# Scatter indices converted one column at a time on ScalarE, and a different pacing of the side work, in an FNet + mixture-of-experts kernel

## The chip, the cores and the metric

The kernel runs on one core of one Trainium2 chip. The metric is the device time in microseconds (us) of that core, the median of three executions without the profiler. A further execution was recorded by the hardware profiler; everything called "the profile" or "the trace" here is that one execution. Its engines are named PE (TensorE, matrix multiplication), PEld (its weight loads), DVE (VectorE), ACT (ScalarE), POOL (GpSimd) and SP (the queue that issues plain DMAs).

## The reference

Two blocks follow each other. The first takes the real part of a two-dimensional Fourier transform of each of eight sequences. The second is a dropless mixture of experts: every row goes to the expert with the largest gate logit, through that expert's two layers, and the result is scaled by the gate's probability.

```
x: (8, 2496, 256)              w_gate: (256, 8)   w1: (8, 256, 1024)   w2: (8, 1024, 256)
X = real(fft(fft(x, axis=1), axis=2)).reshape(19968, 256)
logits = X @ w_gate
e = argmax(logits, 1);  gate = softmax(logits)[row, e]
out[row] = gate * (relu(X[row] @ w1[e]) @ w2[e])
```

All arithmetic is float32.

## The kernel before

**The transform** works batch by batch (b = 0 to 7). `first(b)` folds the input, multiplies it on PE (tile `s`), copies it with ACT (L316) and writes it to a DRAM buffer `Td`. `second(b)` reads it back, makes twice ten tiles of 128 rows in two halves (h = 0, 1), and computes the gate logits beside them; its DVE and ACT steps are L374 to L405.

**Routing.** After each half, `route(b, h)` (L411) finds each row's expert and its place in a DRAM buffer `Xs`, where each expert has a region of its own. The place is made on DVE: `pf` is the float result (L447), and L448 adds a constant that pushes unwanted rows out of bounds and converts to integers, in the tile `pi` (128 x 10, one column for each tile of 128 rows). The ten (index column, row tile) pairs of a half are put in the list `waiting`.

**Scatters.** `send()` takes one pair from that list and issues one indirect DMA on POOL's queue (L230), which writes 128 rows of 1032 bytes to `Xs`. There are 20 for each batch, 160 in all. Results go out through the same queue, and the same line: one indirect DMA `out_dram<-y,ro` for each 128 finished rows.

**The experts.** `experts` takes blocks of rows of one expert from `Xs`: 256 or 128 rows for batches 0 and 1, 512 rows later, at the end 256 and 128 again. `plan(b, ...)` computes on DVE which rows and which expert each block has (tile `p_tab`, L479 to L512); it runs after a batch's last scatter was issued in program order. `fetch` (L517) reads that table into SP's registers and issues three loads: the rows `xb` (L522), which also need the scatters of the batch to have landed, and the expert's two weight matrices. The second layer of a block is eight matmuls for each 128 rows into `py`, evicted by ACT to `y` (L702), then the outgoing DMA. The first layer is a matmul into `ph` with ACT and DVE taking turns to evict it (L684, L682). For 512-row blocks of batches 3 and later (`halved`, L190) the first layer is instead `seven` (L577), which forms a product of 2 x 2 blocks from seven products in place of eight. It has two groups of seven steps, about 0.86 us of PE each; its PSUM tiles `a` and `c` are written twice in a group, so that the second product into `a` waits for ACT's copy L597, and the second into `c` for DVE's L606.

**Order of the work.** All queues are in the order in which the Python code emits instructions; no scheduler changes it. The loop at L804 weaves two generators. `work` (the experts, on the blocks of batch b-1) reports after each piece how much PE work it was (`w`, in units of four 256-wide float32 matmuls, about 1.73 us) and whether it was a piece of `seven` (`full`). `side` is the transform of batches b and b+1, routing and `plan`. Pieces that are not `full` add `TICKS * w / (SHARE * open_)` to `due`, and for each whole unit of `due` the side work moves one step; `SHARE` is thus the part of the round's pieces over which 32 side steps are spread. In rounds b < 4 (`LATE`) each side step is followed by a `send()`. In rounds b >= 4 `send()` is called from L823: `room` grows by `w` with every piece, `full` or not, and each scatter takes `ROOM` = 1.2 from it. A side step that finds `waiting` not yet empty does nothing more than let the next batch's `first` run; `plan` begins once it is empty.

Of the kernel before, what the change touches and what calls it, by code (L numbers as in the profile page):

```python
# [15 lines left out]
ALU = mybir.AluOpType  # L16
# [34 lines left out]
def bc(ap, axis, n):  # L51
    shape = list(ap.shape)
    shape.insert(axis, n)
    return ap[tuple([slice(None)] * axis + [None])].to_broadcast(shape)
# [77 lines left out]
def rounds():  # L132

    want = [((256, 2), (128, 4)), ((256, 4),)] + [((512, B),)] * (B - 2)
    plan, used = [], 0

    def full(done, size):
        return max(0, -(-(done - used - E * (size - 1)) // size))  # L140

    for b in range(B):
        done = (b + 1) * S
        now = []
        for size, most in want[b]:
            k = min(full(done, size), most)
            if k:
                now.append((size, k, False))
            used += size * k
        if b == B - 1:  # L150
            k = full(done, BLK)
            used += BLK * k
            now.append((BLK, k, False))
            now.append((REST, (NT - used + E * (REST - 1)) // REST, True))
        plan.append(now)
    return plan
# [25 lines left out]

TICKS = 32
LATE = 4
SHARE, ROOM = 0.65, 1.2
WARM = 16
MOST = max(k for now in rounds() for _, k, _ in now)

# [1 line left out]
def halved(b, size):  # L190

    return size == 512 and b > 2
# [17 lines left out]
def kernel(ctx: ExitStack, tc, x, w_gate, w1, w2, out):  # L210
    nc = tc.nc
    vec, act, pool = nc.vector, nc.scalar, nc.gpsimd

    def mm(o, lhsT, rhs, start=True, stop=True, **kw):
        nc.tensor.matmul(o, lhsT=lhsT, rhs=rhs, start=start, stop=stop, **kw)  # L215
# [13 lines left out]
    def put_row(dst, idx, rows, last, group):  # L229
        return unordered(pool.indirect_dma_start(  # L230
            out=dst, out_offset=bass.IndirectOffsetOnAxis(ap=idx, axis=0),
            in_=rows, in_offset=None, bounds_check=last, oob_is_err=False), group)


    def sent(ins, b):
        tc.declare_no_dep(ins, group="taken", reason="no block before this batch's round has these rows")
        tc.add_to_no_dep_group(f"xs{b}", ins)
# [25 lines left out]
    con, k = {}, 0  # L263
# [92 lines left out]
    def second(b):  # L356
# [31 lines left out]
        for h in range(2):  # L388
            rows = sp.tile([128, NSL, W], F32, tag="rows", name="rows")
            lg = sp.tile([128, NSL, E], F32, tag="lg", name="lg")  # L390
            for i in range(HW):
                w, k = HW * h + i, 2 * i
                if w + 2 < NG:
                    group(w + 2)
                p3 = pm_.tile([128, 2 * NY + 2 * E + 1], F32, tag="m", name="p3")
                z = zz[:, :, 128 * w:128 * (w + 1)]
                mm(p3[:, 0:NY + 2 * E], z[:, 0], con["rd"][:, 0, 0:NY + 2 * E], True, False, skip_group_check=True)
                mm(p3[:, NY:], z[:, 1], con["rd"][:, 1], False, True, skip_group_check=True)
                zs = sp.tile([128, NY + 1], F32, tag="zs", name="zs")
                act.copy(zs[:], p3[:, NY + 2 * E:])  # L400
                if i:
                    mirror(rows, k - 2)
                vec.tensor_copy(lg[:, k:k + 2], p3[:, NY:NY + 2 * E].rearrange("p (m e) -> p m e", m=2))  # L403
                for m, op in enumerate((ALU.add, ALU.subtract)):
                    vec.scalar_tensor_tensor(rows[:, k + m, 0:NY], p3[:, 0:NY], zs[:, 0:1], zs[:, 1:],  # L405
                                             op0=ALU.add, op1=op)
                yield
            mirror(rows, k)
            yield from route(b, h, rows, lg)

    def route(b, h, rows, lg):  # L411

        nonlocal base

        def small(name, *dims, dt=F32):
            return sp.tile([128, *dims], dt, tag=name, name=name)

        mx, eq, v = small("mx", NSL), small("eq", NSL, E), small("v", NSL)
        vec.reduce_max(mx[:], lg[:], axis=AX_X)
        vec.tensor_tensor(eq[:], lg[:], bc(mx[:], 2, E), op=ALU.is_equal)  # L420
        vec.tensor_tensor(eq[:], eq[:], bc(con["rev"][:], 1, NSL), op=ALU.mult)
        vec.reduce_max(v[:], eq[:], axis=AX_X)
        vec.tensor_tensor(v[:], v[:], con["good"][:, h], op=ALU.mult)
        oh = small("oh", NSL + 1, E, dt=BF16)
        vec.memset(oh[:, NSL], 0.0)
        vec.tensor_tensor(oh[:, 0:NSL], bc(con["rev"][:], 1, NSL), bc(v[:], 2, E), op=ALU.is_equal)
        yield

        su = small("su", NSL)
        vec.tensor_tensor(lg[:], lg[:], bc(mx[:], 2, E), op=ALU.subtract)  # L430
        act.activation(lg[:], lg[:], ACTF.Exp)
        vec.tensor_scalar(rows[:, :, D], con["row"][:, h], float(b * S), None, op0=ALU.add)
        yield

        rk = pm_.tile([128, NSL + 1, E], F32, tag="m", name="rk")
        mm(rk[:], tri[:], oh[:], True, False)
        for s in range(NSL):
            mm(rk[:, s + 1:], ones[:], bc(oh[:, s], 1, NSL - s), False, s == NSL - 1)
        vec.reduce_sum(su[:], lg[:], axis=AX_X)
        vec.tensor_scalar(su[:], su[:], 1e-9, None, op0=ALU.add)  # L440
        vec.reciprocal(rows[:, :, D + 1], su[:])
        yield

        pos, pf, pi = small("pos", NSL, E), small("pf", NSL), small("pi", NSL, dt=I32)
        vec.tensor_tensor(pos[:], rk[:, 0:NSL], bc(base[:], 1, NSL), op=ALU.add)
        vec.tensor_tensor(pos[:], pos[:], oh[:, 0:NSL], op=ALU.mult)
        vec.reduce_sum(pf[:], pos[:], axis=AX_X)  # L447
        vec.tensor_tensor(pi[:], pf[:], con["far"][:, h], op=ALU.add)  # L448
        nxt = cp.tile([128, E], F32, tag="base", name="base", bufs=2)
        vec.tensor_tensor(nxt[:], rk[:, NSL], base[:], op=ALU.add)  # L450
        base = nxt
        for s in range(NSL):
            waiting.append((b, pi[:, s:s + 1], rows[:, s]))

    waiting = deque()

    def send():

        if waiting:
            b, idx, rows = waiting.popleft()  # L460
            sent(put_row(Xs, idx, rows, E * CAP - 1, "xs"), b)


# [255 lines left out]
    def woven(*parts):  # L719
        parts = list(parts)  # L720
        while parts:
            for p in list(parts):
                if next(p, p) is p:
                    parts.remove(p)
                else:
                    yield

    def close(b):

        for size, k, last in rounds()[b]:  # L730
            yield from plan(b, size, k, last)
# [7 lines left out]
    def mixed(b):  # L739

        one, two = (ahead_of(b + 1) if b + 1 < B else iter(())), second(b)
        for _ in range(3):
            next(one, None)
            yield
        for k, _ in enumerate(two):
            if k % 2:
                next(one, None)
            yield
        while waiting:
            next(one, None)  # L750
            yield
        yield from woven(close(b), one)
# [43 lines left out]
    for k, _ in enumerate(second(0)):  # L796
        if k % 2 == 0:
            next(early, None)
        send()
    while waiting:  # L800
        next(early, None)
        send()
    work = experts(todo)
    for b in range(1, B):  # L804

        side, done, due, room = mixed(b), 0, 0.0, 0.0
        if b == 1:
            side = woven(close(0), chain(early, side))
        blocks = [(size, k * size / BIG, halved(b - 1, size)) for size, k, _ in rounds()[b - 1]]
        total = sum(k * (15 if seven_ else 16) for _, k, seven_ in blocks)  # L810
        open_ = sum(k * (8 if seven_ else 16) for _, k, seven_ in blocks)
        while done < total:
            w, full = next(work)
            done += w
            if not full:
                due += TICKS * w / (SHARE * open_) if w else 1
            while due >= 1:
                next(side, None)
                due -= 1
                if b < LATE or not w:  # L820
                    send()
            room = min(room + w, 2)
            if b >= LATE and room >= ROOM:  # L823
                send()
                room -= ROOM
        for _ in side:
            send()
# [52 lines left out]
```

## Time and profile before

| what | value |
|---|---|
| time, three executions | 1330.49, 1332.57, 1944.71 us |
| median | 1332.57 us |
| span of the profiled execution | 1362.3 us |
| mean granted TensorE clock in it | 0.984 |
| rows of PE / DVE / ACT / POOL | 6655 / 1533 / 806 / 335 |
| DMA volume | 249.62 MB, 183 GB/s over the span |

The third execution stands far outside and is used nowhere. In the profiled execution the clock row shows full speed except in a few slices before 380 us, the lowest 0.70 between 68 and 102 us. Each row of the trace gives start and duration of one instruction or of several equal ones (x8), what it writes and reads, and in brackets how long its engine had been idle and what ended the idle time. [...] Matmul ends are modelled, and overlap the next matmul's start.

### The profile page before, as it was taken

The numbers are of one execution on the slowest core, as the hardware profiler recorded it, in microseconds if no ns is written. First come the engines' busy times: TensorE is split into PE (matmuls) and PEld (weight loads), VectorE is DVE, ScalarE is ACT, GpSimd is POOL, SyncE is SP. The second block draws the span as 40 slices with busy tenths as digits, with TensorE's granted clock in tenths as the row PEclk, the third lists the DMA queues.
The fourth block names the chain that finished last, engine by engine and source line by source line (L and its number), as shares of the span: only waits on it lengthen the run. The fifth ranks groups of instructions, "written<-read, shape, count | busy, mean of one in ns | idle before, by whom it ended". The sixth has DMA issues, their size and how long they took to land.

```text
span 1362.3 us, 18852 instructions
## 1 busy us (share of the span) xinstructions
PE 1284.0 (94%) x6655; PEld 1103.7 (81%) x6655; DVE 581.0 (43%) x1533; ACT 368.9 (27%) x806; POOL 326.1 (24%) x335
## 2 busy tenths in 40 slices
PE   6668899899899999999999999999999999999998
PEld 4557888576688888887888878888888889999887
DVE  4553244332456465655366554555545421111211
ACT  1322132132134332432234223332223221111111
POOL 0235215134113411044112521144131111111111
PEclk9869999899999999999999999999999999999999
DMA  8759866644535542454423542232442227777784
GB/s 239 250 214 315 294 239 191 250 127 145 226 93 177 195 170 97 134 177 137 174 109 117 201 184 93 94 131 68 177 182 107 89 96 275 260 259 272 267 318 187
DMA packets 63099, 249.62 MB, mean 183 GB/s; under 512 B 10057, under 2 KB 24883, under 8 KB 43420
## 3 DMA queue, kind: packets, MB, share of 16 engines
q1 hardware_dynamic: 46231, 203.33, 42.6%
q0 software_dynamic: 15888, 42.14, 8.5%
q10 hardware_dynamic: 885, 2.94, 0.7%
q8 instruction: 54, 0.88, 0.3%
q14 instruction: 41, 0.34, 0.1%
HBM read 194.97 MB, written 54.83 MB: 183 GB/s over the span
## 4 chain that ended last, share of the span: by engine, by line
PE 87%; DVE 4%; DMA 3%; issue 3%; another core or an unknown queue 1%; ACT 1%; POOL 0%; SPq 0%; POOLq 0%; DVEq 0%; ACTq 0%
PE py L215 40%; PE ph L215 14%; PE a L215 6%; PE c L215 6%; PE p L215 6%; PE b L215 3%; PE d L215 3%; PE pt L567 3%; PE s L215 3%; PE e L215 3%; DMA xq<-in_x_dram 1%; DMA Td<-t 1%; DMA xb<-Xs 1%; DVE hT L606 0%
## 5 line engine op out<-in xcount | busy, mean ns | idle before, releaser
L215 PE MATMUL py<-w_sb,hT 128*128 128x256 f32 x2560 | 580.2, 381 | 6.3 <-DVE hT L682 4.0
L215 PEld LDWEIGHTS py<-w_sb,hT 128*128 128x128 f32 x2560 | 479.2, 191 | 68.0 <-DVE hT L682 4.6
L230 POOL DMA_INDIRECT out_dram<-y,ro x163 | 159.4, 978 | 890.6 <-ACT y L702 823.9
L215 PE MATMUL ph<-xT,w_sb 128*128 128x128 f32 (+2 forms) x1216 | 221.2, 337 | 8.7 <-issue 4.1
L702 ACT ACTIVATE y<-py,xb 128x256 f32<-128x256 f32 x163 | 77.1, 473 | 521.6 <-PE py L215 505.2
L215 PEld LDWEIGHTS ph<-xT,w_sb 128*128 128x128 f32 x1216 | 178.0, 192 | 40.4 <-issue 19.7
L230 POOL DMA_INDIRECT Xs<-rows,pi x160 | 158.7, 992 | 140.1 <-issue 64.3
L682 DVE TENSOR_SCALAR hT<-ph 128x512 f32<-128x512 f32 x63 | 43.5, 691 | 298.5 <-issue 204.1
L600 DVE TENSOR_TENSOR u<-p,b 128x512 f32<-128x512 f32 x50 | 34.4, 688 | 182.3 <-PE b L215 141.1
L215 PE MATMUL a<-xT,w_sb 128*128 128x256 f32 x400 | 103.3, 381 | 5.0 <-ACT p L597 4.3
L215 PEld LDWEIGHTS a<-xT,w_sb 128*128 128x128 f32 x400 | 75.4, 190 | 17.3 <-ACT p L597 5.5
L568 DVE TENSOR_SCALAR xT<-pt,table 128x512 f32<-128x512 f32 (+1 forms) x94 | 63.2, 673 | 46.1 <-PE pt L567 46.1
L403 DVE COPY lg<-p 128x16 f32<-128x16 f32 x80 | 13.9, 173 | 141.9 <-ACT zs L400 129.9
L215 PE MATMUL s<-xq,w 104*112 104x256 f32 (+2 forms) x208 | 61.7, 421 | 12.0 <-DVE xq L292 11.9
L684 ACT ACTIVATE hT<-ph 128x512 f32<-128x512 f32 x63 | 37.6, 597 | 114.2 <-PE ph L215 78.8
L215 PE MATMUL p<-table,zz 128*128 128x145 f32 (+1 forms) x320 | 58.5, 308 | 10.1 <-issue 5.1
L610 ACT ACTIVATE hT<-a 128x512 f32<-128x512 f32 x50 | 29.9, 597 | 137.2 <-PE a L215 117.0
L215 PEld LDWEIGHTS p<-table,t 120*128 120x128 f32 x352 | 53.7, 203 | 12.6 <-issue 9.2
L567 PE MATMUL pt<-table,xb 128*128 128x128 f32 x326 | 53.3, 279 | 10.8 <-DMA xb<-Xs 9.9
L215 PE MATMUL p<-table,t 120*128 120x120 f32 (+1 forms) x352 | 56.1, 287 | 4.4 <-issue 4.4
L567 PEld LDWEIGHTS pt<-table,xb 128*128 128x128 f32 x326 | 38.6, 142 | 25.8 <-DMA xb<-Xs 11.1
L215 PE MATMUL c<-xT,ws 128*128 128x256 f32 x200 | 52.3, 384 | 7.2 <-DVE hT L606 7.2
(113 smaller groups left out, 1266.3 us busy)
## 6 DMA issues: line engine op xcount, KB each, us to landing
w_sb<-in_moe_w_dram SPq DMA_DIRECT2D x132, 1024.0 KB
xq<-in_x_dram SPq DMA_DIRECT2D x24, 896.0 KB
xb<-Xs SPq DMA_DIRECT2D x28, 516.0 KB
Td<-t SPq DMA_DIRECT2D x18, 448.0 KB
t<-Td SPq DMA_DIRECT2D x8, 768.0 KB
t<-Td SPq DMA_DIRECT2D x8, 640.0 KB
xb<-Xs SPq DMA_DIRECT2D x13, 258.0 KB
xb<-Xs SPq DMA_DIRECT2D x25, 129.0 KB
```

The source lines that it names most:

```text
L215: nc.tensor.matmul(o, lhsT=lhsT, rhs=rhs, start=start, stop=stop, **kw)
L230: return unordered(pool.indirect_dma_start(out=dst, out_offset=bass.IndirectOffsetOnAxis(ap=idx, axis=0), in_=rows, in_offset=None, bounds ...
L403: vec.tensor_copy(lg[:, k:k + 2], p3[:, NY:NY + 2 * E].rearrange("p (m e) -> p m e", m=2))
L567: nc.tensor.transpose(pt[:, c, t], xb[:, 2 * h + t, c * 128:(c + 1) * 128], ident[:])
L568: vec.tensor_scalar(xT[:, :, 256 * h:256 * h + 128 * n], pt[:].rearrange("p c t k -> p c (t k)"), con["alt"][:], None, op0=ALU.mult)
L600: vec.tensor_tensor(u2[:], p1[:], b[:], op=add)
L610: act.activation(h11, a[:], ACTF.Relu)
L682: vec.tensor_scalar(o, ph[:], 0.0, None, op0=ALU.max)
L684: act.activation(o, ph[:], ACTF.Relu)
L702: act.activation(y[:], py[:], ACTF.Copy, scale=xb[:, i, D + 1:D + 2])
```

## The change

Three edits are made.

1. `SHARE` goes from 0.65 to 0.6, in all rounds.
2. For b >= 4 `route` leaves the places as floats in `pf`, and the conversion to integers is no longer the DVE instruction L448 (which still adds the constant) but a copy on ACT of one column, 128 x 1, emitted by `send()` just ahead of that column's scatter. These are 20 copies for each of batches 4 to 7.
3. For b >= 4 a piece that is not `full` adds 0.75 w to `room` in place of w.

```diff
-SHARE, ROOM = 0.65, 1.2
+SHARE, ROOM = 0.6, 1.2
...
-        vec.tensor_tensor(pi[:], pf[:], con["far"][:, h], op=ALU.add)
+        vec.tensor_tensor(pf[:] if b >= LATE else pi[:], pf[:], con["far"][:, h], op=ALU.add)
...
-            waiting.append((b, pi[:, s:s + 1], rows[:, s]))
+            waiting.append((b, pf[:, s:s + 1], pi[:, s:s + 1], rows[:, s]))
...
-            b, idx, rows = waiting.popleft()
+            b, place, idx, rows = waiting.popleft()
+            if b >= LATE:
+                act.copy(idx, place)
             sent(put_row(Xs, idx, rows, E * CAP - 1, "xs"), b)
...
-            room = min(room + w, 2)
+            room = min(room + (w if full else 0.75 * w), 2)
```

## The prediction

> **What bounds the kernel now.** I read the page first: engine sums and slices.
>
> ```profile
> PE 1284.0 (94%) x6655; PEld 1103.7 (81%) x6655; DVE 581.0 (43%) x1533; ACT 368.9 (27%) x806; POOL 326.1 (24%) x335
> PE   6668899899899999999999999999999999999998
> POOL 0235215134113411044112521144131111111111
> ```
>
> PE is the bound, and the change takes no matmul away; it can only give back time in which PE waits for others. These gaps lie in the first ten slices and, small, in the slices with POOL digits 4 and 5, the scatter stretches. So I asked what PE and its weight loads waited for between 430 and 945 us (rounds 4 to 7):
>
> ```profile
> PE c L215 <- DVE hT L606: 5.5, 8, 1.2
> PE a L215 <- ACT p L597: 4.3, 3, 1.7
> ...
> PEld c L215 <- DVE hT L606: 8.7, 8, 1.6
> PEld a L215 <- ACT p L597: 5.5, 3, 2.1
> ```
>
> Columns are total, times, longest, in us. PE gets stuck in the first layer behind late evictions. Why late, the timeline of one such stretch tells, POOL, DVE and ACT in turn:
>
> ```profile
> 596.53 1.10 POOL L230 DMA_INDIRECT Xs<-rows,pi  x1 [0.30 <-issue]
> 597.93 0.97 POOL L230 DMA_INDIRECT Xs<-rows,pi  x1 [0.30 <-issue]
> 599.21 1.01 POOL L230 DMA_INDIRECT Xs<-rows,pi  x1 [0.30 <-issue]
> 600.52 0.97 POOL L230 DMA_INDIRECT Xs<-rows,pi  x1 [0.30 <-issue]
> ...
> 598.69 0.68 DVE L546 TENSOR_TENSOR ws<-ws,w_sb 128x512 f32<-128x512 f32 x1
> 601.47 0.69 DVE L600 TENSOR_TENSOR u<-p,b 128x512 f32<-128x512 f32 x1 [2.10 <-PE d L215]
> ...
> 599.34 0.57 ACT L597 COPY p<-a 128x512 f32<-128x512 f32 x1
> 602.96 0.60 ACT L610 ACTIVATE hT<-a 128x512 f32<-128x512 f32 x1 [3.05 <-PE a L215]
> ```
>
> L600 needs product b (598.75 + 1.03) and ACT's copy (ended 599.91), yet starts at 601.47, 1.5 us late; ACT's L610 is 0.6 late. Just before, scatters had run back to back, one each 1.28 us, eight DMAs from 591.4. Rounds 4 to 7 each have two such runs (436, 591, 748, 900 and, with two short breaks, 460, 616, 772, 922), and DVE is about 0.8 to 1.6 us late near the end of every one. In runs of four or five it was not, nor in blocks without scatters. I take it that a long unbroken run of POOL's DMAs delays the other engines' starts; how, the trace doesn't say.
>
> Last the chain of waits, at the two large gaps in front of new blocks:
>
> ```profile
> 237.01 0.97 POOL Xs L230
> 238.29 0.97 POOL out_dram L230
> 239.26 0.30 issue
> 239.56 2.33 DMA Xs<-rows,pi
> ...
> 242.07 3.39 DMA xb<-Xs
> ...
> 345.59 0.17 DVE p_tab L501
> ...
> 347.34 3.54 DMA xb<-Xs
> ```
>
> At 245.5 PE had been idle for 6.6 us: the block's rows waited for batch 2's last scatter, last in a POOL backlog. At 350.9 it had been idle for 3.5: the load waited for the block table, made too late on DVE.
>
> [...] the scatter of 239.56 is off POOL at 240.53, and SP goes on at 241.89. So I add some 2.3 us from a scatter's start to its landing.
>
> **Part 1: paced scatters, rounds 4 to 7.** Before, a scatter waits only for its half's indices and for the queue; a program position behind an outgoing DMA then lets the next seven go at once. Now each needs an ACT copy which stands, in ACT's order, between the evictions of its place: in a first layer two behind L597, one behind L615, and so on. With 1.2 units of 1.73 us each, a scatter comes each 2.1 us on average; in a second layer 1.2 / 0.75 x 1.73 = 2.8 us, plus an outgoing DMA each 3.46. No run should exceed three or four. Gain: the waits above are 5.5 + 4.3 + 1.1 of smaller rows = 10.9 us on PE, 17.6 with weight loads (8.7 + 5.5 + 3.4 of smaller ones, without the transposes' usual 0.4). PE's modelled ends hide part of each wait, the weight loads overstate it. I take **13**, bounds 0 (if pace isn't what matters) and 17.6.
>
> Costs. 80 copies: the nearest rows are L367's, 128 x 5 or 6, 0.16 to 0.18 us, so 80 x 0.17 = 14 us of an ACT that is idle for 73%. In `seven` ACT has five instructions of 0.6 in 6 us, and the reuse of `a` leaves about 0.9; 0.17 or 0.34 fits: nothing. POOL's rows stay 320; DVE's L448 stays. The first copy of a half waits for `route`'s end on DVE, and queued behind it are `zz`'s eviction L374 or the next `y`. POOL waited up to 2.3 us at that place. PE then works on a `py` tile of 3.46 us, so I take 0.13 each, eight times: **1**; bounds 0 and 18.4.
>
> **Part 2: SHARE, rounds 4 to 7.** Side steps come 8% sooner, in the same PE amount. By the program's order one thing crosses a border: the first 9 DVE steps of `route` for h = 1, and ACT's exponential, now stand before the third block's first layer, not after it. Lengths from 607.4 to 609.2: 1.8 us. From the rows at 591 to 597: rows done 592.2, exponential at 593.9, `t` copied to 594.75, L597 to 595.3, then L600, L603, L606 at 0.69 each to 597.5, where product c's second use stood at 597.0. So 0.5 a round, **2** in all; bounds 0 and 1.3 x 4 = 5. Queues: SP's input load and `Td` write of that step move up as well, 9 units before anyone needs them; nothing.
>
> **Part 3: SHARE, rounds 1 to 3.** POOL's order there, counted in scatters (s) between outgoing DMAs (o):
> - Round 1: o 9s, later o 3s o 3s, becomes o 10s, later o 3s o 1s. ACT and DVE were released about 1.3 us after these runs (130.5 and 145.4), PE standing 2.3 and 4.0 us. One DMA more costs 1.28, two fewer return 2.56: **+1.3**.
> - Round 2: 9s o 3s o 1s becomes 10s o 1s. The last scatter is 4 DMAs earlier and one later, 3 x 1.28 = 3.8 us. ACT's release moves by 1.28, and with it the outgoing DMA ahead of that scatter; some of it is lost: **+2.5** of the 6.6.
> - Round 3: the table's DVE steps come three units of 1.73 us earlier, ending at 340.6 in place of 345.8; the last scatter (338.78) is two DMAs earlier and lands near 338.5. With the 5.1 us from table to landed rows that the chain shows, `xb` is there at 345.7, before PE is ready at 347: +3.5. The long run at 294 grows by one: -1.3. **+2.2**.
> Together 6; bounds -4 (all runs worse, no gap closed) and 12.
>
> **Sum**: 13 - 1 - 2 + 6 = 16 us off the span of 1362.3, 1.2%. The timed runs are 30 us shorter than the span; granted clock 0.984 explains 22 of it, so the waits should mostly be in them too. 1332.6 - 16 = **1317**. Two per cent, 26.7 us, is about what a measurement of this kernel can tell from no change.
>
> **The rivals.**
> - *The delay follows the number of scatters, not their crowding.* All 20 a batch remain. For it: lateness appears only with scatters about. Against: runs of four or five show none. Part 1 gains 2 at best, the rest 6 - 3: 1332.6 - 5 = 1328.
> - *Slower: the copies hold ACT.* Each half's first copy waits for DVE's place, with evictions behind it. If PE gets all of the 2.3 us that POOL waited, 8 x 2.3 = 18.4, plus 2 for `route`, against only 6 from rounds 1 to 3 and 4 of the pacing: 1332.6 + 10 = 1343. It decides once a hold exceeds a `py` tile's slack, about 3 us from the copy's turn. Against: ACT's waits for `py` in second layers are near 3 us a tile.
> - *More returns than I count.* All 17.6, 12 from the early rounds, no costs: 1303.
> - *The change doesn't do it*: POOL bunches up again because copies of one step come in pairs and outgoing DMAs add to them; gains and costs cancel: 1331.
>
> **How the numbers follow.** Chances: forecast 0.55 (1309 to 1324), count of scatters 0.17, no effect 0.08, held ACT 0.12, more 0.08. Leaving out the upper half of the slower case and the far end of the last one, 1303 to 1338 holds 8 in 10. Faster than by 2% (below 1306) takes nearly everything: 0.09. Slower by 2% (above 1359) needs more than the whole price of the held ACT: 0.04. Within: 0.87.
>
> **What would show it.** Between 430 and 945 us: no run of over four of POOL's DMAs, PE's waits for L606 and L597 near zero, L600 and L614 starting within 0.2 us of their product. ACT rows 886. In front of the new blocks: xb waits of about 4 and 0 us. I am wrong if delays appear at 2 us spacing, or if PE waits for a ScalarE that waits for L448 or L430.

## The result, and the profile after

The changed kernel takes 1321.22 us (median of six runs, 1318.93 to 1324.04) against 1331.38 us before. The ratio is 0.9929 with a 95% interval of 0.9911 to 0.9946, so it is faster by 0.7%, some 9.4 us. (The six executions of before include the one of 1944.71 us; the ratio leaves it out.) That is 4 us from the forecast and inside its range, but the reason is another one than the forecast's main term.

The first page of the changed kernel answers to the lines shown of before. I add its clock row:

```profile
span 1318.3 us, 19009 instructions
...
PE 1271.6 (96%) x6655; PEld 1101.3 (84%) x6655; DVE 583.1 (44%) x1533; ACT 374.5 (28%) x886; POOL 329.4 (25%) x335
...
PE   5759999999999999999999999999999999999998
POOL 0335225043114411143113511153311111111111
PEclk6869999999999999999999999999999999999999
```

The 80 new ACT rows are there. The span fell by 44 us, far more than the timed runs did. That alone says that something in the profiled execution of before is not in the timed ones. Between 430 and 945 us (rounds 4 to 7) PE's waits shrank to one row:

```profile
PE p L215 <- ACT t L367: 0.6, 3, 0.2
```

This looks like the forecast coming true. What contradicts it is POOL's rows in the earlier rounds of the same trace. From 204.2 to 226.9 us 18 indirect DMAs follow each other there without a break; the last of them:

```profile
218.30 0.98 POOL L230 DMA_INDIRECT Xs<-rows,pi  x1 [0.30 <-issue]
219.58 0.97 POOL L230 DMA_INDIRECT Xs<-rows,pi  x1 [0.30 <-DMA Xs<-rows,pi]
220.86 0.97 POOL L230 DMA_INDIRECT Xs<-rows,pi  x1 [0.30 <-issue]
222.14 0.98 POOL L230 DMA_INDIRECT Xs<-rows,pi  x1 [0.30 <-issue]
223.42 0.97 POOL L230 DMA_INDIRECT out_dram<-y,ro  x1 [0.30 <-ACT y L704]
224.70 0.97 POOL L230 DMA_INDIRECT Xs<-rows,pi  x1 [0.31 <-issue]
225.97 0.97 POOL L230 DMA_INDIRECT out_dram<-y,ro  x1 [0.30 <-issue]
```

PE works through this stretch without a gap, and no ACT or DVE row beside it starts late. A run twice as long as those blamed in the prediction does no harm here. These rounds have no `seven`, so the stronger test is a second profile of the kernel before.

Two theories went into the experiments. **A**, the prediction's: long unbroken runs of POOL's DMAs delay DVE and ACT, and the paced scatters remove that. **B**: those delays belong to the one profiled execution of before, and the gain comes from SHARE in rounds 1 to 3, where the rows of new blocks arrive earlier. In the later experiments a further question was whether a gap of PE costs more than its own length. "With clock" means there that the granted clock is about half for a while behind a gap of PE, as in the second profile of before (0.50 from 232 to 236 us and 0.78 from 236 to 240, behind a gap of 4.4 us); "without", that a gap costs its length alone. What the half clock costs was there the author's estimate; the measured cost stands below.

### The profile page after: what moved, and what is told of

The parts are those of the page before. It is cut to its first block, busy times and chain, and to the rows that moved or that the text cites. A ratio compares the mean times of both kernels' runs of the same rounds, so it can differ in the third digit from the quotient of the medians.

```text
span 1318.3 us, 19009 instructions
## 1 busy us (share of the span) xinstructions
PE 1271.6 (96%) x6655; PEld 1101.3 (84%) x6655; DVE 583.1 (44%) x1533; ACT 374.5 (28%) x886; POOL 329.4 (25%) x335
## 5 line engine op out<-in xcount | busy, mean ns | idle before, releaser
L230 POOL DMA_INDIRECT Xs<-rows,pi x160 | 162.3, 1014 | 174.8 <-DVE rows L405 52.5
L215 PEld LDWEIGHTS s<-xq,w 104*112 104x112 f32 x208 | 38.2, 201 | 21.4 <-DVE xq L292 10.2
```

What stands on the lines that cost most here:

```text
L230: return unordered(pool.indirect_dma_start(out=dst, out_offset=bass.IndirectOffsetOnAxis(ap=idx, axis=0), in_=rows, in_offset=None, bounds ...
```

## The experiments

Each ratio is against the kernel before, run on the same chip, with its 95% interval.

**The kernel before once more**, unchanged, for a second profile.

> The kernel before, unchanged, profiled a second time. Theory A (long unbroken runs of POOL's DMAs delay DVE and ACT): the second profile again has a span near 1362 us, with DVE or ACT 0.8 to 1.6 us late at the end of each of the eight runs between 430 and 945 us, and PE waiting some 11 us there. Theory B (those delays belong to that one profiled execution; the kernel's own losses lie in rounds 1 to 3): span near 1331 us, as the timed runs, no late starts in the same runs of DMAs, PE waits below 3 us between 430 and 945 us, while the waits for the rows of new blocks (6.6 and 3.5 us) are still there. Time ratio 1.000 in both.

It measured 0.9992 (0.9977 to 1.0007), and its profile has a span of 1329.5 us. The same run of eight DMAs of round 5 as in the prediction, POOL first, then DVE:

```profile
577.62 1.09 POOL L230 DMA_INDIRECT Xs<-rows,pi  x1 [0.30 <-issue]
579.02 0.97 POOL L230 DMA_INDIRECT Xs<-rows,pi  x1 [0.30 <-issue]
580.30 1.01 POOL L230 DMA_INDIRECT Xs<-rows,pi  x1 [0.30 <-issue]
581.61 0.97 POOL L230 DMA_INDIRECT Xs<-rows,pi  x1 [0.30 <-issue]
...
579.77 0.68 DVE L546 TENSOR_TENSOR ws<-ws,w_sb 128x512 f32<-128x512 f32 x1
581.03 0.69 DVE L600 TENSOR_TENSOR u<-p,b 128x512 f32<-128x512 f32 x1 [0.57 <-ACT p L597]
```

L600 follows L546 after 1.26 us here, where the first profile had 2.78, and L600 starts as soon as ACT's copy is done. POOL's DMAs are as crowded as before. At these rows the first profile is 18.9 us behind the second, at the end 32.8. The stretches from 430 to 945 us of the first and second profile (length, then busy time and rows of PE, PEld, DVE, ACT, POOL, the clock, DMA):

```profile
430.00:945.00 515.00, 503.23 (x2567) 437.31 (x2566) 275.30 (x661) 171.77 (x365) 142.24 (x145) 1.00 0.41 143
...
430.00:945.00 515.00, 514.70 (x2641) 452.89 (x2640) 293.96 (x729) 171.30 (x363) 137.30 (x140) 1.00 0.41 146
```

PE stands for 11.8 us in the first, for 0.3 us in the second. Theory A falls. What had held up DVE and ACT in that one execution stays open.

What the second profile keeps is the two waits for the rows of new blocks. PE's waits between 100 and 430 us (total, times, longest; so one of 4.4 us and one of 3.6):

```profile
PE pt L567 <- DMA xb<-Xs: 8.0, 2, 4.4
```

**The parts one by one.** SHARE alone, the ACT copies alone, the room alone:

```diff
# SHARE alone
-SHARE, ROOM = 0.65, 1.2
+SHARE, ROOM = 0.6, 1.2
# copies alone: the edits in route and send(), SHARE and room as before
+            if b >= LATE:
+                act.copy(idx, place)
# room alone
-            room = min(room + w, 2)
+            room = min(room + (w if full else 0.75 * w), 2)
```

> Only SHARE 0.6 in place of 0.65. Theory A: about a third of the change's gain, ratio 0.997 or above, since the runs of DMAs in rounds 4 to 7 stay. Theory B: nearly the whole gain of the change, ratio near 0.993, from rounds 1 to 3, where the last scatter and the block table come earlier.

> Only the ACT copies, SHARE 0.65, room counted as before. Theory A: scatters of rounds 4 to 7 follow the evictions, no late starts, ratio near 0.995 or below. Theory B: ratio 1.000 within 0.001, since there is nothing to remove.

> Only the 0.75 w in pieces that are not full; places are converted on DVE, SHARE 0.65. Theory A: the seven scatters behind an outgoing DMA still run back to back, so ratio 0.999 to 1.000. Theory B: 1.000.

SHARE alone gives 0.9926 (0.9907 to 0.9946), the copies 0.9992 (0.9978 to 1.0006), the room 0.9998 (0.9984 to 1.0011). The first two are as theory B has it; the room doesn't tell the theories apart. Within these intervals the whole change is SHARE. The copies cost nothing that can be measured, and bring nothing: their profile lacks the runs of eight in rounds 4 to 7, but there was no delay to remove.

**SHARE in one round.**

```diff
-                due += TICKS * w / (SHARE * open_) if w else 1
+                due += TICKS * w / ((0.6 if b == 2 else SHARE) * open_) if w else 1
# and, in another kernel, b == 3
```

> SHARE 0.6 in round 2 alone. Theory B, with clock [...]: the gap of 4.6 us at 227 shrinks to about 1.2, [...] a wait of rk for DVE of about 1.5 us comes in [...]: 3.5 to 5.5 us less, ratio 0.996 to 0.997. Theory B without clock (gaps cost their length only): 1.5 to 2 us less, ratio 0.9985 or above.

> SHARE 0.6 in round 3 alone. With clock: the gap of 3.8 us at 330 closes [...] 6 to 7 us less, ratio near 0.995. Without clock: 3 to 3.8 us less, ratio near 0.9975. Theory A: slower, since the long run of scatters at 281 grows by two.

Round 2 alone gives 0.9969 (0.9956 to 0.9982), about 4.1 us; round 3 alone 0.9951 (0.9939 to 0.9963), about 6.5 us. Their product, 0.9920, leaves nothing for rounds 1 and 4 to 7 within the intervals. Round 3's gap was 3.6 us long, and closing it is worth more than that even at the near end of its interval (4.9 us). The windows around the two gaps tell why. Second profile of before, then the changed kernel, around the first gap:

```profile
227.00:232.00 5.00, 0.61 (x4) 0.21 (x2) 0.69 (x1) 0.00 (x0) 0.00 (x0) 0.89 0.56 199
232.00:238.00 6.00, 6.00 (x17) 4.99 (x18) 0.75 (x1) 0.00 (x0) 0.00 (x0) 0.52 1.01 421
...
229.00:231.00 2.00, 1.02 (x7) 0.59 (x6) 0.69 (x1) 0.00 (x0) 0.00 (x0) 1.00 1.01 354
231.00:237.00 6.00, 6.00 (x33) 5.33 (x32) 2.45 (x4) 0.47 (x1) 0.97 (x1) 1.00 1.02 424
```

The third number from the end is the granted clock, and (x17) counts PE's rows. After a gap of 4.4 us the next six microseconds run at 0.52 and hold 17 matmul rows; after a gap of 1.0 us they run at full clock and hold 33. Six microseconds at half clock are three lost: from the new block's first transposes to its next ones it takes 6.78 us in the one profile and 3.95 us in the other, for the same sixteen matmuls in between.

```profile
232.85 6.03 PE L215 MATMUL py<-w_sb,hT 128*128 128x256 f32 x16
...
231.20 3.62 PE L215 MATMUL py<-w_sb,hT 128*128 128x256 f32 x16
```

The same stands after the second gap, at 334 us:

```profile
330.00:334.00 4.00, 0.81 (x2) 0.00 (x0) 0.69 (x1) 0.00 (x0) 0.00 (x0) 0.91 0.63 216
334.00:340.00 6.00, 5.61 (x16) 4.62 (x17) 0.75 (x1) 0.00 (x0) 0.00 (x0) 0.50 1.00 405
```

The profile of round 2 alone has the second gap, 3.5 us, without the half clock:

```profile
326.00:330.00 4.00, 0.78 (x6) 0.76 (x7) 0.53 (x2) 0.00 (x0) 0.00 (x0) 1.00 0.87 312
330.00:336.00 6.00, 6.00 (x32) 5.28 (x31) 2.79 (x6) 0.47 (x1) 0.97 (x1) 1.00 1.03 427
```

So a gap of about this length doesn't always bring it. In all profiles together ten unfilled gaps of 3.3 to 6.6 us stand ahead of these two blocks. Behind nine of them the sixteen matmuls after the transposes took 4.95 to 6.03 us (4.95 and 5.30 in the first profile of before, 6.03 and 6.01 in the second); behind the tenth, and behind gaps of up to 2.7 us, 3.62 us. It was also seen behind a shorter wait: in the profile of SHARE alone PE waits 1.3 us for the routing's `oh`, and a little later runs at half clock (0.50):

```profile
192.00:194.00 2.00, 2.00 (x6) 1.53 (x5) 0.92 (x6) 0.58 (x1) 1.14 (x2) 0.50 0.45 188
```

The changed kernel has the same wait, 1.33 us, and keeps full clock (1.00 from 170 to 204 us).

**Filling the gaps.** If idle time brings the half clock, useless work in the same gap should keep the clock, with the wait itself untouched. (`follow[0]` is the batch of the next block, `b` that of the present one.)

```diff
                 turned = turn(*follow[:2], got[0])
+                if follow[0] in (2, 3) and follow[0] != b:
+                    pw = pse.tile([128, D], F32, tag="d", name="py")
+                    for _ in range(32):
+                        mm(pw[:], ones[:], bc(ones[:], 1, 2))
```

> The kernel before, with 32 matmuls of constants (bf16, 128x256, result unused, [...]) ahead of the transposes of the first blocks of batches 2 and 3, where PE waits 4.6 and 3.8 us for the rows. The waits stay; only PE is no longer idle in them. With clock: no halved clock at 231 and 333, up to 6.8 us less, ratio near 0.995. Without clock: 1.000, or a little slower where a filler is longer than the wait.

It gives 0.9974 (0.9962 to 0.9986), 3.5 us for work that computes nothing (32 matmuls in 3.66 us in its profile). The windows of the first gap, same instants as above:

```profile
227.00:232.00 5.00, 4.18 (x36) 3.41 (x35) 0.69 (x1) 0.00 (x0) 0.00 (x0) 1.00 0.56 193
232.00:238.00 6.00, 6.00 (x32) 5.35 (x33) 2.26 (x4) 0.47 (x1) 0.97 (x1) 1.00 1.02 419
```

The rows arrive at the same time (the transposes begin at 231.90, against 231.94), and the six microseconds after it hold 32 rows in place of 17. Behind the second gap the six microseconds from 332 us run at 1.00 too, where the second profile of before had 0.50. In this profile the half clock went with the idle time. The 3.5 us are half of the 6.8 us that were hoped for, an estimate of the author's. Part of that lies in the hope, since the windows above give 2.8 us a gap; and the half clock doesn't follow a gap in every execution. How often it does in the timed ones isn't known.

**A lower SHARE in the early rounds only.**

```diff
+                due += TICKS * w / ((0.55 if b < LATE else SHARE) * open_) if w else 1
```

> SHARE 0.55 in rounds 1 to 3, 0.65 in rounds 4 to 7, no ACT copies. Batch 2's last scatter then stands ahead of the outgoing DMA and the table of batch 3 is ready three more units earlier. Theory B: both gaps closed, the small cost in rounds 4 to 7 gone; 1 to 3 us below the changed kernel, ratio to before 0.990 to 0.992. Theory A: as the kernel before or slower, runs of scatters up to 13 long.

0.9938 (0.9915 to 0.9962): no better than 0.6, and not the further gain that theory B foretold. Both gaps are closed in its profile (0.6 us of wait is left), but PE's waits, same columns, have another one in round 2, for the routing on DVE (`rk` is the routing's matmul):

```profile
PE rk L215 <- DVE oh L426: 3.1, 1, 3.1
```

In the changed kernel the same row is 1.3 us. Behind the 3.1 us the granted clock falls to 0.50 (188 to 190 us). The side work stands earlier in PE's program order, and PE stands there until DVE has made its input: 3.1 us here. I take it that this is what bounds SHARE from below; no run takes this wait away.

**Combinations**, in search of a faster version: round 3 at 0.6 with the filler ahead of batch 2's block; rounds 2 and 3 at 0.6 with fillers at the start; round 3 with both fillers.

```diff
# fillers at the start, ahead of and behind the first block's transposes
+                pw = pse.tile([128, D], F32, tag="d", name="py")
+                for _ in range(32):
+                    mm(pw[:], ones[:], bc(ones[:], 1, 2))
                 for xT in turn(b, size, got[0]):
                     pass
+                for _ in range(16):
+                    mm(pw[:], ones[:], bc(ones[:], 1, 2))
```

> SHARE 0.6 in round 3 alone, and the 32 constant matmuls in front of batch 2's first block only, where PE waits 4.5 us. With clock: the 6.9 us of round 3 alone [...] without the wait for routing that SHARE 0.6 brings into round 2: ratio 0.992 to 0.994, as the changed kernel. Without clock: 0.995, as round 3 alone.

> SHARE 0.6 in rounds 2 and 3 alone, and constant matmuls at the start: 32 where PE waits 7.3 us for the first block's rows (78 us), 16 where it then waits 3.2 us for the first weights. With clock: the first layer from 89 us on runs at full clock sooner, 2 to 4 us more than the sum of rounds 2 and 3: ratio 0.988 to 0.991. Without: 0.992, as the two rounds together.

> Round 3 at 0.6, constant matmuls in front of batch 2's first block and at the start (the two before it together, without SHARE 0.6 in round 2). With clock: 0.989 to 0.992. Without: 0.995.

They give 0.9920 (0.9899 to 0.9942), 0.9920 (0.9899 to 0.9940) and 0.9921 (0.9900 to 0.9943). None is told apart from the changed kernel. The first and the third come out at the edge of "with clock" and clear of "without". Round 3 alone was 0.9951, so round 2's gain seems to be had by the filler in place of SHARE as well, though the intervals just touch. The second misses its "with clock" and comes out where "without" had it. Its profile has full clock from about 82 us after the span's start, where the changed kernel has it from about 94, and nothing that can be measured comes of it. The traces show why in part: the first block's transposes begin at 85.02 us with the filler, at 85.01 in the changed kernel, since their rows come no sooner; and in round 2 PE waits 2.7 us for rows in place of 1.0. I take it, without a run that shows it, that the start is paced by the 20 scatters of batch 0 (53 to 81 us in the changed kernel) and the loads behind them.

## Why the prediction was right or wrong

- **Time**: 1317 forecast, 1321.22 measured; 16 us less forecast, about 9.4 measured. The direction was right; the sum came out well by luck, from two errors of opposite sign.
- **Part 1, 13 us from paced scatters: wrong.** The copies alone are worth 0.9992. The step that failed is the first reading: waits in one profiled execution (10.9 us on PE, priced at 13) were taken as those of the kernel. The trace of before was read rightly, and late starts did stand at the end of each long run; but the second profile has the same runs and no late starts, and PE stands for 0.3 us there. The signs that the prediction named came true (no run over four, no waits for L606 and L597, 886 ACT rows) and prove nothing, since the kernel before has no such waits in its second profile either. The prediction had the warning in its hands. The span was 30 us longer than the timed runs; it put 22 of that on a granted clock of 0.984 and went on. The second profile, with a lower clock of 0.973, is just 1329.5 us long, so the clock wasn't the cause.
- **Cost of the copies, 1 us: right within what can be measured.** They took 0.192 us each in the median (estimated 0.17), and PE's waits between 430 and 945 us hold no ACT copy.
- **Part 2, 2 us lost in rounds 4 to 7**: not seen in the time; rounds 2 and 3 alone explain the whole of SHARE. The wait for L606 that it foretold isn't among PE's waits in the changed kernel.
- **Part 3, 6 us: the mechanism right, the size too small.** Round 1, +1.3 forecast; no run has it alone, but SHARE's gain leaves about 0 for it: the waits it was to change were those of the odd execution. Round 2, +2.5 against 4.1. The mechanism was read from the chain and the traces agree: the last scatter starts 5.0 us before PE is through with the old block in the changed kernel, 1.6 us before in the second profile, and the wait fell from 4.4 to 1.0 us. That is 3.4 us, between the 3.8 worked out and the 2.5 counted. Round 3, +2.2 against 6.5: the block table came earlier, the load was issued at 320.15, 6 us before PE needed its rows, and PE never waited. (The gap read as 3.5 us is 3.3 on PE in the first profile, 3.6 in the second.) What the sum missed is the half clock behind each gap, some 2.8 us apiece in the second profile; and in round 3 it charged 1.3 for a longer run that costs nothing. With this term the traces give 3.4 + 2.8 less the new wait of 1.3 for the routing, 4.9, for round 2, and 3.6 + 2.8 = 6.4 for round 3.
- **The rivals**: the rival that the change doesn't do what it says came nearest for the scatters, for a reason that it didn't name: they became paced, but there was nothing to gain. The other three did not occur: no delay follows the number of scatters either, no wait of PE is for one of ACT's copies, and the gain is smaller than forecast, not larger.

## What to carry to other kernels

When a profiled execution is longer than the timed ones, take a second profile before pricing its waits: here 11.8 us of waits, tidy and repeated in four rounds, were not in the kernel's usual run. As an estimate from the ten gaps of 3.3 to 6.6 us in these traces, price a TensorE gap of that length at its length and up to 3 us of half clock behind it (2.8 us in the second profile of before), and look at the granted clock in the windows after a gap, after shorter ones too; filling two such gaps with useless matmuls was worth about a third of the whole change here. Split a change into its parts on the chip before believing its description: one constant out of three edits was all of the gain, and the edit with most code in it none.

## What the runs showed of the hardware

- Unbroken runs of POOL's indirect DMAs at 1.28 us each stand beside DVE, ACT and PE rows that don't start late: eight in the second profile of before, 18 in the changed kernel. The late starts of the first profile stay unexplained.
- Half clock followed nine of ten gaps of PE of 3.3 to 6.6 us: sixteen matmuls took 4.95 to 6.03 us in place of 3.62. In the second profile of before it was 0.52 over the six us from 232 us, behind 4.4 us, and 0.50 over those from 334 us, behind 3.6 us. It is missing after 3.5 us in the profile of round 2 alone, and it came after shorter waits for the routing too: 1.3 us in that of SHARE alone, 3.1 us in that of SHARE 0.55.
- With useless matmuls in the two gaps, the profile shows a clock of 1.00 behind both, with the rows of the first block no later (231.90 against 231.94 us).
- A scatter's row on POOL lasts 0.97 us (median of 160 in the changed kernel); the last scatter ahead of batch 2's first block landed 2.33 us after its start, in both profiles of before.
- An ACT copy of 128 x 1 from float32 to int32 takes 0.174 to 0.195 us in the changed kernel.
